# A forward transform folded at its thirds in an RWKV and Hyena kernel

## The chip, the cores and the metric

The kernel runs on one core of a Trainium2 chip. TensorE (PE) multiplies matrices into PSUM, VectorE (DVE), ScalarE (ACT) and GpSimd (POOL) do the elementwise work, and SyncE's queue (SP) issues the DMAs. The metric is the device time of one execution in microseconds (us); lower is better.

## The reference

Four sequences of 768 steps, 8 heads of 48 channels, so 384 channels in all. The first half is a linear recurrence with a decaying state per head:

```python
for t in range(S):
    cur = np.einsum('bhd,bhe->bhde', u[None] * kt, vt)
    y[:, :, t] = np.einsum('bhd,bhde->bhe', rt, state + cur)
    state = wt[:, :, :, None] * state + np.einsum('bhd,bhe->bhde', kt, vt)
```

Its output `x` (4 x 768 x 384) goes through a gated long convolution along the sequence, written with Fourier transforms:

```python
proj = x @ w_proj                      # three groups of 384 columns: x1, x2, x3
X2 = np.fft.rfft(x2, n=S, axis=1)
H = np.fft.rfft(filter_fft, n=S, axis=0)[None]
x2_conv = np.fft.irfft(X2 * H, n=S, axis=1)
return ((x1 * x2_conv * x3) @ w_out).astype(np.float32)
```

## The kernel before

**Recurrence.** Each sequence is cut into 6 chunks of 128 steps, 24 chunks in all. For a chunk, four loads bring `w`, `k`, `r`, `v` (192 KB each, rings of six buffers). ACT takes the logarithm (`lw`), PE sums it along the steps (`cs`, `ce`), ACT exponentiates (`en`, `enp`, `eq`, `eqp`). `q`/`qp` and `kh`/`khp` scale `r` and `k`; `tqk` transposes them on PE and `tT` copies them out; `sc` multiplies them, `mt` masks the result (or `ma` copies it and `mm` masks it on POOL). `kv` and `S` carry the state. The bonus term with `u` is `rk`, `rku`, a sum `cc` and a product `vc`. `y` collects the chunk's output in PSUM. It ends in one of two ways: `y` and then `xn`, in which DVE adds `vc`, or `yb`, in which a further matmul with the identity adds `vc` in PSUM, and then `xc`, a plain copy. `yt` transposes it and `xT` copies it to SBUF.

**Convolution.** The transform of 768 steps is split into halves first: `sa` and `sb` (lines 631 to 641) add and subtract chunk `ci` and chunk `ci` - 3, which gives a sum half and a difference half of 384 steps, kept with channels on the partitions in `sd_b`. `x2` (L679) projects each third (128 steps) of each half with `w_proj`; `ab` copies it to `ab_b`. `f` (L690) multiplies by the table `F` of sines and cosines, in six slots a sequence, three thirds a slot. Slots 0, 1, 4 and 5 are one group of 128 rows each and take one matmul of 384 columns per third; slots 2 and 3 hold two groups of 64 rows (`mid`) and take two half-wide matmuls per third. `da` and `db` (or a copy `X` and then `ua`, `ub`) multiply by the transformed filter, `pp` adds, `i1` and `i2` (L719) transform back, `ec`, `s`, `d` put the halves together (`d` writes its output backwards), `yy` multiplies by the gate. The gate is made from `p1`, `p3` (L648), `x1` and `g` or `gc` and `gm`. `po` (L761) multiplies by `w_out`, `o` copies, `st` stores.

**Set-up.** The filter is loaded once (`ldfilt`, 1152 KB), halved by `fs` and `fd` (L384 to L388) and transformed by `hf` with the helper `fwd` (L390), which `f` uses too; `rsc` (L339) scales a small table `rot`, on which the steps `ht` and `hr` wait. `z` and `zs` are matmuls on zeros whose result nobody reads.

**Order.** The whole program is one list, `ORDER` (L37). A word is an engine, an operation and its arguments, and for PE the PSUM bank: `P:f0.1@2` is `f` of sequence 0, slot 1, into bank 2, `A:ab0.1.2` a copy on ACT. Each engine runs its words in this order. A word can name DVE (`V`), ACT or POOL (`G`) for the same operation. A POOL word with "!" also waits for the latest DVE word whose operation is in the set `shut` (L803); this is called a turn below, and `rsc` is not in the set. Most operations run through helpers, so in the profile L231 is any copy on ACT and L232 any copy on another engine.

Of the kernel before, what the change touches and what calls it, by code (L numbers as in the profile page):

```python
# [37 lines left out]
S:ldw0 V:mem0 G:iorot! G:mke! G:iota! P:zs29@0 A:tLn S:ldw2 A:lw0 S:ldw1 S:ldr0 G:mki! S:ldk0 A:lw2  # L38
S:ldu V:mem2 V:mem4 V:mem3 V:ang1 V:mem1 V:ang2 V:ang0 A:lw1 V:angn P:cs0@0 P:ce0@1 P:z3@2 P:z7@3
A:enp0 P:ce1@2 S:ldfilt A:eq0 P:zs1@3 G:mkd! G:rk0! G:uc! S:ldk2 P:zs8@1 V:mem5 V:rku0 V:khp0 P:z2@3  # L40
P:cs1@1 A:sin P:cs2@4 P:z1@3 V:q0 S:ldk1 P:zs1@5 V:fs S:ldv0 A:enp2 A:ph1 A:enp1 P:zs2@3 P:zs2@5
P:tqk0@5 V:mem6 G:fd! P:hf0@3 V:rsc V:cc0 V:khp2 P:mtr0@0 P:hf1@4 A:tT0 A:ht0.0 P:ce2@5 P:sc0@8
# [6 lines left out]
V:mt2 A:lw5 A:ht2.1 A:xc1 V:cc3 P:ce5@2 V:S2 G:vc2! P:hf5@4 S:ldw6 S:ldv3 A:tT3 S:ldk5 S:ldr5
P:yb2@3 P:cs5@0 S:ldv4 G:q4! P:tqk4@5 V:hr2.0 V:hr2.1 P:sc3@8 V:xc2 A:v3 P:kv3@4 P:yt1@3 G:rk4!  # L50
G:vc3! G:rku4! A:eqp5 A:en5 S:ldw7 S:ldp1 A:tT4 A:lw6 A:xT1 A:v4 S:ldr6 G:kh5! P:zs2@0 A:xT0 G:rk5!
V:mt3 P:yb3@0 P:yt2@5 P:ce6@3 A:xc3 V:S3 P:sc4@8 A:eq6 A:lw7 V:cc4 G:vc4! V:qp5 P:tqk5@4 P:kv4@2
G:rku5! P:zs1@0 P:cs6@1 V:mt4 P:yt3@0 P:y4@3 A:tT5 V:S4 G:wc1! V:sa3 A:enp6 S:ldv5 A:xT3 A:xT2 V:xn4
P:sc5@8 S:ldk6 V:cc5 P:yt4@3 P:x20.0.0@4 G:q6! V:mt5 A:v5 V:sa4 P:ce7@5 A:ab0.0.0 V:khp6 G:vc5!
V:sb3 A:hb2 V:sb4 P:y5@2 G:rk6! S:ldw8 P:x20.0.1@4 S:ldr7 A:eq7 P:tqk6@1 A:lw8 P:x20.1.0@0 S:ldv6
V:xn5 P:cs7@5 P:yt5@2 A:ab0.0.1 P:x20.1.1@4 V:tT6 A:ab0.1.0 V:sa5 P:sc6@8 P:x20.0.2@0 A:xT4 P:cs8@3
V:sb5 A:v6 A:xT5 G:q7! G:rku6! A:ab0.0.2 P:ce8@1 S:ldk7 A:en7 A:en8 S:ldp0 A:ab0.1.1 P:f0.1@2
P:x20.1.2@0 G:rk7! V:mt6 S:ldk8 G:kh7! P:f0.0@5 A:ab0.1.2 V:cc6 V:db0.0 S:ldv7 A:eq8 V:rku7 P:kv6@4
P:f0.4@3 V:S6 P:f0.5@0 A:wc0 P:f0.2@1 G:vc6! G:kh8! V:da0.2 P:tqk7@4 V:db0.2 V:cc7 V:da0.0 G:v7!
S:ldr8 P:p10.1.0@3 G:rk8! P:p10.2.0@2 P:kv7@0 A:tT7 S:ldw10 A:x10.2.0 V:S7 P:sc7@8 P:p10.1.1@4  # L60
# [29 lines left out]
P:po0.4@1 A:eqp17 S:ldw23 S:st0.2 A:xT13 V:da1.2 A:o0.3 A:lw18 P:yt12@3 A:o0.4 A:xT12 P:sc16@8  # L90
V:qp17 P:f1.1@2 G:mm15! P:yt14@4 G:vc15! P:cs18@0 A:lw20 G:v16! G:kh17! V:S15 V:mt16 V:cc16 G:pp1.2!
S:ldr22 S:ldv20 P:yb15@5 G:rk17! S:ldr21 V:db1.0 S:st0.0 S:ldk22 P:tqk17@3 A:xT14 P:kv16@1 A:en18
A:xc15 P:p12.2.0@4 V:S16 A:tT17 P:p32.2.0@0 P:p12.0.0@2 P:ce18@1 P:sc17@8 P:yt15@3 A:x12.2.0
A:x12.0.0 A:eq18 P:ce20@4 V:pp1.0 V:pp1.1 V:rku17 V:sa15 A:v18 V:g2.2.0 G:kh18! G:vc16! A:xT15
A:eq20 P:p32.1.0@2 P:cs20@1 P:y16@5 P:i21.1@0 A:gc2.1.0 G:q18! P:p12.1.0@4 V:sb15 V:mt17 A:en20
A:v17 A:ec1.1 V:cc17 A:x12.1.0 V:gm1.1.1 V:q20 V:xn16 P:x22.1.0@2 P:i21.0@1 A:ec1.0 A:ab2.1.0
G:vc17! P:tqk18@0 P:i21.2@4 P:y17@1 V:tT18 V:xn17 G:kh20! P:kv18@5 V:S18 V:rk18 P:yt16@2 A:lw19
P:ce19@3 P:i11.0@0 A:ec1.2 P:yt17@1 A:xT16 A:eq19 P:cs19@4 V:sb16 A:en19 P:sc18@8 P:tqk20@3 V:d1.0
V:sa16 A:xT17 G:rku18! V:s1.0 A:v19 V:sb17 A:tT20 A:lw21 P:x22.1.1@4 P:i11.2@5 P:p32.1.1@2
G:gm1.2.1! V:sa17 A:gc2.1.1 V:d1.2 G:rk20! V:s1.2 P:p12.1.1@0 P:i11.1@3 V:mt18 A:ab2.1.1 G:q19!  # L100
P:x22.1.2@1 P:cs21@2 P:ce21@4 P:x22.0.0@5 G:kh19! A:x12.1.1 A:enp21 V:cc18 V:d1.1 A:eq21 A:ab2.0.0
A:lw22 A:ab2.1.2 P:x22.0.1@0 P:p32.0.0@4 V:s1.1 P:tqk19@5 P:p32.2.1@3 P:sc20@8 P:kv19@1 V:khp21
P:f2.5@2 V:g2.0.0 P:p12.0.1@4 A:ab2.0.1 G:vc18! G:rk19! P:x22.0.2@0 A:gc2.2.1 A:tT19 P:y18@5
A:x12.0.1 A:lw23 A:v20 S:ldr23 S:ldk23 P:f2.4@3 P:cs23@4 A:ab2.0.2 A:en23 V:yy1.0 V:yy1.2 V:yy1.1
V:S19 V:db2.2 V:mt20 P:ce22@1 P:po1.0@2 P:po1.4@0 A:eq22 P:sc19@8 G:rku19! P:cs22@1 G:q21! G:rku20!
S:ldv23 S:ldv21 A:o1.0 V:da2.2 V:cc19 P:tqk21@2 A:enp22 V:xn18 P:po1.2@3 G:rk21! P:po1.5@4 P:f2.1@5
V:khp22 S:ldv22 A:o1.4 P:yt18@1 P:po1.3@0 A:tT21 P:ce23@2 A:o1.2 P:kv20@3 G:q22! A:xT18 A:o1.5
# [25 lines left out]
def kernel(  # L133
# [506 lines left out]
    def op_sb(e, c):  # L640
        return two(e).tensor_sub(*sums(e, c, 1))  # L641
# [222 lines left out]
```

## Time and profile before

| | us |
|---|---|
| three runs | 160.06, 159.96, 159.25 |
| median | 159.96 |
| the profiled execution | 159.13 |
| its span, first to last instruction | 157.4 |

The profile is of one execution. Its page gives the busy time of each engine, the granted clock of PE in 40 slices of the span, the chain of work that ended last, and the costliest groups of instructions by line. A group's row reads: line, engine, operation, output and input with their shapes, count, busy us and mean ns of one, then idle time before them and what ended it. Rows of waits read: engine and line, what it waited for, us in total, how often, and the longest. Rows of the timeline and the chain begin with the start in us and the duration. PE's matmuls are pipelined, so the start of the next one tells more of their cost than the duration of one. In the first 30 us the 16 DMA engines were busy for 0.91 of the time.

### The profile page before, as it was taken

The numbers are of one execution on the slowest core, as the hardware profiler recorded it, in microseconds if no ns is written. First come the engines' busy times: TensorE is split into PE (matmuls) and PEld (weight loads), VectorE is DVE, ScalarE is ACT, GpSimd is POOL, SyncE is SP. The second block draws the span as 40 slices with busy tenths as digits, with TensorE's granted clock in tenths as the row PEclk, the third lists the DMA queues.
The fourth block names the chain that finished last, engine by engine and source line by source line (L and its number), as shares of the span: only waits on it lengthen the run. The fifth ranks groups of instructions, "written<-read, shape, count | busy, mean of one in ns | idle before, by whom it ended". The sixth has DMA issues, their size and how long they took to land.

```text
span 157.4 us, 4146 instructions
## 1 busy us (share of the span) xinstructions
PE 142.6 (91%) x1541; PEld 92.8 (59%) x1544; DVE 136.6 (87%) x264; ACT 126.0 (80%) x261; POOL 111.0 (71%) x134
## 2 busy tenths in 40 slices
...
PEclk9997559999999999999999999999999999999999
...
GB/s 102 203 277 184 215 170 201 209 251 191 236 210 145 265 160 213 186 203 218 179 252 189 158 205 196 187 226 216 218 138 200 0 4 2 0 0 4 329 240 233
...
## 3 DMA queue, kind: packets, MB, share of 16 engines
...
q8 instruction: 12, 0.20, 0.5%
q14 instruction: 8, 0.07, 0.1%
...
## 4 chain that ended last, share of the span: by engine, by line
PE 58%; ACT 10%; DVE 8%; DMA 8%; POOL 5%; issue 5%; SPq 3%; ACTq 0%; DVEq 0%; POOLq 0%
PE p L651 13%; PE x L682 6%; PE po L764 6%; DMA ldk<-in_k_dram 5%; PE f L402 5%; PE tqk L540 4%; PE i L722 4%; PE sc L553 3%; PE f L395 3%; SPq L450 2%; DMA ldw<-in_w_dram 2%; PE y L606 2%; PE ce L466 2%; DVE rot L340 2%; ACT xT L231 2%
## 5 line engine op out<-in xcount | busy, mean ns | idle before, releaser
L651 PE MATMUL p<-xT,wproj 128*128 128x384 bf16 x144 | 29.0, 326 | 0.0
L521 POOL TENSOR_TENSOR rk<-ldr,ldk 128x384 bf16<-128x384 f32 x23 | 23.0, 1002 | 7.4 <-DMA ldk<-in_k_dram 3.1
L560 DVE TENSOR_TENSOR mt<-sc,mask_excl 128x1024 bf16<-128x1024 f32 x22 | 26.7, 1216 | 0.5 <-PE sc L553 0.4
L231 ACT ACTIVATE qkT<-tqk 128x1024 bf16<-128x1024 bf16 x21 | 21.6, 1027 | 2.4 <-PE tqk L540 1.7
L534 POOL TENSOR_TENSOR vc<-v,cc 128x384 bf16<-128x384 bf16 x24 | 19.8, 831 | 3.8 <-ACT v L231 1.5
L518 POOL TENSOR_TENSOR qk<-ldr,eq 128x384 bf16<-128x384 f32 x17 | 17.0, 1001 | 3.0 <-ACT eq L485 3.0
L651 PEld LDWEIGHTS <-wproj 128*128 128x128 bf16 x144 | 12.8, 98 | 7.3 <-DVE sd L641 0.3
L540 PE MATMUL tqk<-ident,qk 128*128 128x128 bf16 x192 | 15.4, 223 | 1.1 <-DVE qk L502 1.1
L682 PE MATMUL x<-wproj,sd 128*128 128x384 bf16 x72 | 15.0, 326 | 1.0 <-ACT ab L231 0.6
L524 POOL TENSOR_TENSOR rku<-rk,u_bc 128x384 bf16<-128x384 bf16 x15 | 13.7, 915 | 2.7 <-DVE y L756 1.5
L722 PE MATMUL i<-m_b,P 128*128 128x384 bf16 x72 | 15.0, 326 | 0.0
L764 PE MATMUL po<-wout,y 128*128 128x384 bf16 x72 | 14.5, 326 | 0.5 <-DVE y L756 0.3
L540 PEld LDWEIGHTS <-qk 128*128 128x128 bf16 x192 | 12.1, 99 | 4.6 <-DVE qk L502 1.7
L456 ACT ACTIVATE lg<-ldw 128x384 bf16<-128x384 f32 x24 | 12.6, 524 | 2.5 <-DMA ldw<-in_w_dram 2.5
L514 POOL TENSOR_TENSOR qk<-ldk,en 128x384 bf16<-128x384 f32 x12 | 12.0, 1002 | 2.4 <-ACT x L231 2.0
L231 ACT ACTIVATE ab<-x 128x384 bf16<-128x384 f32 x24 | 11.4, 495 | 2.5 <-PE x L682 2.3
L527 DVE TENSOR_REDUCE cc<-rku 128x8 f32<-128x384 bf16 x24 | 12.9, 541 | 0.0
L231 ACT ACTIVATE x<-p 128x384 bf16<-128x384 f32 x24 | 11.6, 501 | 0.7 <-PE p L651 0.7
L231 ACT ACTIVATE xT<-yt 128x384 bf16<-128x384 bf16 x23 | 11.0, 494 | 1.0 <-DVE sd L638 0.8
L589 DVE TENSOR_TENSOR S<-kv,eq 128x384 bf16<-128x384 f32 x20 | 11.0, 550 | 0.8 <-PE kv L581 0.7
L710 DVE TENSOR_TENSOR UA<-f,T 128x768 bf16<-128x768 f32 x11 | 10.4, 949 | 0.3 <-PE f L395 0.3
L677 POOL TENSOR_TENSOR g<-g,x 128x384 bf16<-128x384 bf16 x8 | 7.2, 913 | 4.7 <-DVE g L677 2.6
...
## 6 DMA issues: line engine op xcount, KB each, us to landing
...
```

Source lines behind the costliest of these rows:

```text
L231: return nc.scalar.activation(out=o, in_=i, func=AF.Copy)
L518: return two(e).tensor_mul(qk_b[c % 3][:, 0, :, 0:D], ld["r"][c % LD], eq)
L521: return two(e).tensor_mul(rk_b[c % 2], ld["r"][c % LD], ld["k"][c % LD])
L524: return two(e).tensor_mul(rku_b[c % 2], rk_b[c % 2], u_bc)
L527: nc.vector.tensor_reduce(out=cc_b[c % 3], in_=rku_b[c % 2], axis=AX.X, op=ALU.add)
L534: return two(e).tensor_mul(vc_b[c % 3], v_b[c % 4], cc_b[c % 3].to_broadcast([L, H, D]))
L540: nc.tensor.transpose(p[:, x, j, :], qk_b[c % 3][:, x, 2 * j:2 * j + 2, :], ident)
L560: nc.vector.tensor_mul(mt_b[c % 3], bank_of[f"sc{c}"].rearrange("p q j t -> p (q j) t"), dataclasses.replace(m[:, :], ap=[m[:, :].ap[0], [ ...
L651: nc.tensor.matmul(p, wproj[:, n, cb, fb * L:(fb + 1) * L], xT_b[b % 2][:, cb, sl], start=(cb == 0), stop=(cb == CB - 1),)
L682: nc.tensor.matmul(p, sd_b[q][:, cb, ti * L:(ti + 1) * L], wproj[:, 1, cb, :], start=(cb == 0), stop=(cb == CB - 1),)
L722: nc.tensor.matmul(p, P_b[b % 2][:, s // 2, s % 2, cb * L:(cb + 1) * L], m_b[:, s].rearrange("p a t -> p (a t)"), start=(i == 0), stop=(i ...
L764: nc.tensor.matmul(p, y_b[0][:, cb, ti * L:(ti + 1) * L], wout[:, cb, :], start=(cb == FIRST[0]), stop=(cb == FIRST[-1]),)
```

## The change

The sines and cosines of a half sequence are symmetric or antisymmetric about its middle. So the first third and the mirrored last third are added (`fp`) or subtracted (`fm`) before the projection; slots 0, 2 and 5 need the sum, slots 1, 3 and 4 the difference, and all need the middle third as it is. `x2` still makes three products a half: sum, middle, difference. `f` then takes two of them a slot instead of three. `sa` and `sb` of a sequence's last chunk write their 128 steps backwards, so that `fp` and `fm` read plain slices.

```diff
+    fo_b = ring("fo", 2, [L, 2, CB, L], BF16)
...
+    EVEN = (0, 2, 5)
...
-        return sd_b[q][:, :, (ci - NT) * L:(ci - NT + 1) * L], lo, hi
+        o = sd_b[q][:, :, (ci - NT) * L:(ci - NT + 1) * L]
+        if ci == NCH - 1:
+            o = dataclasses.replace(
+                o, offset=o.offset + (L - 1) * o.ap[-1][0],
+                ap=list(o.ap[:-1]) + [[-o.ap[-1][0], L]],
+            )
+        return o, lo, hi
...
+    def op_fp(e, b, q):
+        return two(e).tensor_add(
+            fo_b[q][:, 0], sd_b[q][:, :, 0:L], sd_b[q][:, :, 2 * L:3 * L],
+        )
+
+    def op_fm(e, b, q):
+        return two(e).tensor_sub(
+            fo_b[q][:, 1], sd_b[q][:, :, 0:L], sd_b[q][:, :, 2 * L:3 * L],
+        )
...
             nc.tensor.matmul(
-                p, sd_b[q][:, cb, ti * L:(ti + 1) * L], wproj[:, 1, cb, :],
+                p, sd_b[q][:, cb, L:2 * L] if ti == 1 else fo_b[q][:, ti // 2, cb, :],
+                wproj[:, 1, cb, :],
                 start=(cb == 0), stop=(cb == CB - 1),
             )
...
     def op_f(e, b, s, bank):
-        fwd(f"f.{b}.{s}", bank, s, ab_b[0][:, 0], ab_b[0][:, 1])
+        p = ps(f"f.{b}.{s}", bank)
+        side = 0 if s in EVEN else 2
+        for ti, j in ((1, 1), (0, side)):
+            if s in (2, 3):
+                for q in (0, 1):
+                    nc.tensor.matmul(
+                        p[DP * q:DP * q + DP, :], mid(ti, s, q), ab_b[0][:, q, j, :],
+                        start=(ti == 1), stop=(ti == 0),
+                    )
+            else:
+                nc.tensor.matmul(
+                    p, slot_cols(ti, s), ab_b[0][:, s // 4, j, :],
+                    start=(ti == 1), stop=(ti == 0),
+                )
...
     shut = {"kh", "q", "rk", "rku", "vc", "v", "ua", "ub", "pp", "yy", "gm", "wc",
-            "fs", "fd", "hb", "ang", "angn", "he", "uc"}
+            "fs", "fd", "hb", "ang", "angn", "he", "uc", "rsc", "fp", "fm"}
```

The whole of `ORDER` is written anew, 1088 words before and 1094 after: another order on every engine, other banks, and other engines for some operations. The words whose number on an engine differs, without those where two engines only differ by one:

| operation | before | after |
|---|---|---|
| `fp`, `fm` | none | 11 DVE, 5 POOL |
| `yb` with `xc`; `y` with `xn` | 9; 15 | 16; 8 |
| `xc` | 8 ACT, 1 DVE | 16 ACT |
| `rku` | 9 DVE, 15 POOL | 16 DVE, 8 POOL |
| `rk` | 1 DVE, 23 POOL | 3 DVE, 21 POOL |
| `q`, `qp` | 2 and 5 DVE, 17 POOL | 3 and 1 DVE, 20 POOL |
| `eq`, `eqp` (both ACT) | 19, 5 | 23, 1 |
| `xT` | 1 DVE, 23 ACT | 4 DVE, 20 ACT |
| `g`; `gc` with `gm` | 12 DVE; 12 ACT, 4 DVE and 8 POOL | 14 DVE; 10 ACT, 5 DVE and 5 POOL |
| `o` | 2 DVE, 22 ACT | 24 ACT |
| `mc` | 3 DVE | 1 DVE, 2 ACT |
| `fd` | POOL | DVE |
| `z`, `zs` matmuls | 21, 46 | 7, 33 |

The loads begin in another order: before `ldw0 ldw2 ldw1 ldr0 ldk0 ldu ldfilt ldk2 ldk1 ldv0`, after `ldw1 ldw2 ldw0 ldu ldfilt ldk1 ldr1 ldk0 ldv0 ldr0`. On DVE, `rsc` and `fd` follow `fs` directly, and `rk1`, `q1` and `rku1` stand among the set-up that comes next.

More of the change, by code (lines that the diff above doesn't have):

```diff
@@ L37 @@
 ORDER = """
[L38 to L42, printed above, removed]
@@ L49 @@
[L49 to L54, printed above, removed]
@@ L55 @@
[L55 to L60, printed above, removed]
@@ L90 @@
[L90 to L95, printed above, removed]
@@ L96 @@
[L96 to L107, printed above, removed]
@@ L126 @@
-V:d3.1 P:poa3.5@2 P:poa3.2@4 A:o2.3 P:poa3.1@5 S:st2.5 V:yy3.1 P:pob3.5 P:pob3.0 P:pob3.2 P:poa3.4@1
-S:st2.0 P:poa3.3@3 A:o3.5 P:pob3.3 P:pob3.4 S:st2.1 S:st2.4 S:st2.3 A:o3.0 S:st3.5 V:o3.2 S:st3.0
-S:st3.2 P:pob3.1 A:o3.1 A:o3.4 A:o3.3 S:st3.1 S:st3.4 S:st3.3
+S:ldw1 S:ldw2 G:iota! G:mki! G:iorot! S:ldw0 A:tLn A:lw2 V:mem3 V:mem1 G:mke! A:lw1 V:ang1 S:ldu
+V:ang2 V:ang0 V:mem0 V:angn V:mem4 P:cs2@0 V:mem6 P:ce2@1 S:ldfilt A:en2 P:zs29@2 A:lw0 P:ce1@2
+G:uc! G:mkd! V:mem5 V:fs S:ldk1 A:sin S:ldr1 S:ldk0 S:ldv0 S:ldr0 P:z7@0 P:zs2@0 P:ce0@3 P:hf0@0
@@ new lines @@
+P:cs1@4 V:rsc P:zs2@5 P:cs0@5 A:eq1 A:en1 A:eq0 A:ht0.1 A:v0 P:hf1@2 V:fd S:ldr3 P:hf2@4 P:hf3@3
+A:enp0 A:ht0.0 V:rk1 V:q1 V:mem2 V:hr0.1 A:ht1.1 G:kh1! V:khp0 V:hr0.0 P:kv0@5 S:ldk3 V:hr1.1 G:q0!
+A:eqp2 P:tqk0@0 V:S0 P:hf4@5 A:ht1.0 G:rk0! S:ldw3 V:rku1 P:tqk1@4 S:ldk2 S:ldr2 A:he P:hf5@2 G:rk3!
+A:lw3 A:ph2 V:tT0 P:ce3@0 V:cc1 S:ldv1 V:rku0 A:ht2.1 S:ldw4 A:tT1 V:hr1.0 V:cc0 P:cs3@3 P:sc0@8
+G:kh2! V:hr2.1 G:vc0! P:mtr1@4 V:qp2 P:tqk2@1 G:rk2! A:enp3 A:ht2.0 A:ms1 V:mt0 A:v1 S:ldw5 S:ldv2
+P:kv1@5 A:tT2 V:rku3 V:rku2 V:hr2.0 P:sc1@8 P:mtr0@1 P:yb0@2 S:ldr4 S:ldk4 A:lw4 A:eq3 G:hb2! V:khp3
@@ new lines @@
+P:yb4@2 P:yt3@5 P:yt2@4 G:rk6! A:lw8 A:xc4 P:ce7@1 V:S4 A:xT2 V:mt5 A:eq7 V:sa3 V:sb3 A:xT3 G:vc5!
+P:y5@0 V:xn5 P:ce8@2 P:yt4@4 A:wc1 P:yt5@0 G:kh6! V:sb4 V:sa4 A:eq8 G:rku6! P:tqk6@5 V:sb5 V:sa5
+A:xT5 A:en7 P:x20.1.1@1 S:ldv6 P:x20.0.1@2 G:v6! A:hb1 S:ldk7 V:fp0.1 P:x20.1.0@0 V:fm0.0 V:fp0.0
+S:ldr7 A:ab0.0.1 A:ab0.1.1 A:ab0.1.0 V:fm0.1 S:ldp0 P:x20.0.2@3 P:x20.0.0@2 V:tT6 A:ab0.0.2 V:cc6
+G:rk7! A:ab0.0.0 P:sc6@8 P:kv6@0 P:f0.5@1 P:cs8@3 P:x20.1.2@2 V:q7 V:rku7 A:xT4 V:db0.2 G:kh7! A:wc0
+P:f0.0@4 P:f0.2@5 S:ldk8 A:en8 G:vc6! P:tqk7@1 S:ldr8 G:q8! G:rk8! A:ab0.1.2 A:tT7 P:p10.2.1@3
@@ new lines @@
+P:po0.2@2 A:o0.5 V:da1.2 G:rk17! P:f1.3@4 P:f1.2@5 A:tT16 P:sc15@8 G:q17! S:ldk22 P:yb14@3 S:ldv21
+S:ldk21 P:kv16@0 A:lw18 A:o0.4 G:rku17! G:vc16! S:ldv19 S:ldv20 P:ce18@1 A:ma15 P:sc16@8 V:da1.1
+V:db1.1 A:lw19 P:po0.3@5 G:mm15! A:xc14 P:yt14@3 P:ce19@4 V:mt16 V:xT14 A:eq18 A:o0.2 P:po0.0@1
+A:o0.3 V:S16 G:vc15! G:v17! P:f1.1@2 P:tqk17@5 P:p12.0.0@3 A:lw20 V:db1.0 P:yb15@0 A:o0.0
+P:p12.2.0@1 G:q18! S:ldr22 V:gm1.1.1 S:ldv23 S:st0.4 A:eq19 P:cs18@2 P:cs20@4 V:rk18 A:tT17
+A:x12.0.0 P:sc17@8 V:pp1.1 P:yb16@3 A:enp18 V:pp1.0 S:st0.1 V:pp1.2 V:rku18 A:xc15 A:en20 V:khp18
```

123 lines of the change are left out of this document (70 added, 53 removed).

## The prediction

> **What bounds the kernel now.** I read the page first, then the busy time in three stretches, then each engine's waits inside the middle one, then the start.
>
> ```profile
> span 157.4 us, 4146 instructions
> PE 142.6 (91%) x1541; PEld 92.8 (59%) x1544; DVE 136.6 (87%) x264; ACT 126.0 (80%) x261; POOL 111.0 (71%) x134
> PEclk9997559999999999999999999999999999999999
> PE 58%; ACT 10%; DVE 8%; DMA 8%; POOL 5%; issue 5%; SPq 3%; ACTq 0%; DVEq 0%; POOLq 0%
> ...
> 0.00:30.00 30.00, 21.94 (x199) 14.18 (x202) 19.73 (x53) 19.97 (x36) 14.47 (x30) 0.83 0.91 195
> 30.00:140.00 110.00, 108.39 (x1272) 72.06 (x1274) 106.37 (x193) 98.85 (x210) 93.17 (x103) 1.00 0.79 169
> 140.00:157.40 17.40, 12.30 (x75) 6.59 (x71) 10.46 (x20) 7.19 (x16) 3.32 (x3) 0.99 0.50 182
> ```
>
> The columns of the last three rows are stretch, length, busy time of PE, PEld, DVE, ACT and POOL, then granted clock, DMA share and GB/s. The chain of work that ended last is 58% PE, so at first sight a matmul saved is time saved. The middle stretch says otherwise: of 110 us DVE is busy 106.37, ACT 98.85 and POOL 93.17. PE's 108.39 is modelled and hides small gaps. DVE has 110 - 106.37 = 3.6 us to give; no saving on PE can bring more in this stretch unless DVE's own work falls.
>
> POOL looks free with 17 us idle. Its waits and DVE's rows in the same stretch show that it is not:
>
> ```profile
> POOL rk L521 <- DVE y L756: 2.7, 1, 2.7
> POOL g L677 <- DVE rku L524: 2.1, 1, 2.1
> POOL qk L514 <- ACT x L231: 2.0, 1, 2.0
> ...
> L756 DVE TENSOR_TENSOR y<-SD,g 128x768 bf16<-128x768 bf16 x8 | 4.2, 558 | 0.0
> L716 DVE TENSOR_TENSOR P<-UA,UB 128x768 bf16<-128x768 bf16 x6 | 3.1, 552 | 0.0
> L524 DVE TENSOR_TENSOR rku<-rk,u_bc 128x384 bf16<-128x384 bf16 x5 | 1.8, 353 | 0.0
> L677 DVE TENSOR_TENSOR g<-g,x 128x384 bf16<-128x384 bf16 x3 | 1.0, 349 | 0.0
> ```
>
> The first two waits are for DVE instructions whose result POOL does not use: the program makes each POOL word marked "!" wait for the latest DVE instruction of the set `shut` (a turn). The four DVE groups, in the same window, take 4.2 + 3.1 + 1.8 + 1.0 = 10.1 us, so POOL and turns hold 93.17 + 10.1 = 103.3 of 110 us. PE, DVE and POOL-with-turns are all at 94% or more.
>
> The start is different: there single waits are long.
>
> ```profile
> 15.31 2.61 POOL L388 TENSOR_TENSOR UA<-filt 128x1152 bf16<-128x1152 f32 x1 [4.51 <-DVE UA L385]
> 15.38 2.56 DVE L340 TENSOR_TENSOR rot<-rot,rsc 128x12 f32<-128x12 f32 x1
> ...
> DVE UA L385 <- DMA filt<-in_moe_filter_fft_dram: 1.7, 1, 1.7
> ACT E L420 <- DVE rot L340: 4.2, 1, 4.2
> L323 DVE TENSOR_SCALAR o<-tcol 128x3 int32<-128x3 f32 x1 | 0.2, 169 | 0.0
> ```
>
> Twelve elements took 2.56 us, while a POOL instruction of 2.61 us had begun 0.07 us earlier. The nearest small DVE row, 169 ns, says what `rot` costs alone.
>
> **The change part by part.** Durations, from the groups by line and the chain in order of time:
>
> ```profile
> 137.19 0.49 PE f L402 x3
> 138.65 0.61 PE f L395 x6
> ...
> L395 PE MATMUL f<-ab,F 128*64 128x384 bf16 x48 | 5.4, 334 | 0.0
> L598 PE MATMUL y<-vc,ident 128*128 128x384 bf16 x9 | 3.0, 328 | 0.3 <-POOL vc L534 0.3
> L638 DVE TENSOR_TENSOR sd<-xT,yt 128x384 bf16<-128x384 bf16 x12 | 4.1, 350 | 0.4 <-ACT eq L485 0.2
> L618 DVE TENSOR_TENSOR xn<-y,vc 128x384 bf16<-128x384 f32 x15 | 8.2, 550 | 0.8 <-PE y L606 0.7
> L385 DVE TENSOR_TENSOR UA<-filt 128x1152 bf16<-128x1152 f32 x1 | 1.4, 1359 | 1.7 <-DMA filt<-in_moe_filter_fft_dram 1.7
> L231 ACT ACTIVATE xn<-y 128x384 bf16<-128x384 f32 x8 | 4.0, 495 | 0.2 <-PE y L606 0.2
> L231 ACT ACTIVATE xT<-yt 128x384 bf16<-128x384 bf16 x23 | 11.0, 494 | 1.0 <-DVE sd L638 0.8
> L524 POOL TENSOR_TENSOR rku<-rk,u_bc 128x384 bf16<-128x384 bf16 x15 | 13.7, 915 | 2.7 <-DVE y L756 1.5 <-DVE rk L521 0.6 <-DVE g L677 0.5
> L641 POOL TENSOR_TENSOR sd<-xT 128x384 bf16<-128x384 bf16 x1 | 0.9, 910 | 0.1
> L753 DVE TENSOR_TENSOR SD<-i,E 128x384 bf16<-128x384 f32 x12 | 6.6, 552 | 0.3 <-issue 0.3
> L744 DVE TENSOR_TENSOR SD<-i,E 128x384 bf16<-128x384 f32 x12 | 6.6, 550 | 0.0
> L508 DVE TENSOR_TENSOR qk<-ce,ldr 128x384 bf16<-128x384 f32 x5 | 2.7, 548 | 0.0
> L518 POOL TENSOR_TENSOR qk<-ldr,eq 128x384 bf16<-128x384 f32 x17 | 17.0, 1001 | 3.0 <-ACT eq L485 3.0
> ...
> 133.51 0.87 ACT L231 ACTIVATE xT<-yt 128x384 bf16<-128x384 bf16 x2
> ```
>
> *PE.* Three full `f` matmuls take 0.49, so one is 0.163; sixteen go (four slots of four sequences, one each): 2.6 us. Six half-wide ones take 0.61, so a pair is 0.20; eight pairs go: 1.6 us. The new order also makes `yb` of seven more `y`: seven bonus matmuls at 0.163, +1.1. Net -3.1 us of PE time, spread evenly.
>
> *DVE.* Counted from the two orders. In: eleven folds (`fp`, `fm`) at 0.35, as `sd`, 3.9; seven `rku` from POOL, 2.5; `fd` 1.36; `rk`, `q`, `xT`, `g`, `gm`, `ub` about 4.7. Out: seven `xn` at 0.55, 3.9; four `qp` 2.2; one `mt` 1.2; `da`, `o`, `xc`, `ec`, `sa`, `mc`, `ms`, `hb` about 4.8. Net +0.3 us: nothing. `rot` loses its 2.4 us beyond, in the start.
>
> *ACT.* Eight more `xc` 4.0, three fewer `xT` -1.5, and single moves of `mc`, `ms`, `wc`, `ma`, `o`, `ec`, `X`, `v` against two `gc`: +7.6 us of isolated durations; about +6 where they run back to back (two `xT` take 0.87, not 0.99). 98.85 + 6 of 110 still fits.
>
> *POOL.* Seven `rku` (-6.4), `fd` (-2.6), `gm`, `rk`, `wc` out; five folds at 0.91 (+4.6), `q`, `sa`, `mm` in: about -4.9. Against it stand new turns: eleven folds, seven `rku` and three `rk`/`q` on DVE, 3.9 + 2.5 + 1.65 = 8.0 us. POOL with turns: about +3.
>
> *The reversed sums.* `sa`/`sb` of the last chunk, eight instructions, write backwards. Before has a reversed write in `d` and a forward one in `s`, each 0.55, but with a float32 input. Bounds: 0 and 8 x (0.55 - 0.35) = 1.6 us; I take 0, since the `d` row is the nearest. [...]
>
> *Start.* `fd` goes to DVE, behind `rsc`: `rot` is no longer beside a POOL instruction, -2.4 us on DVE. `filt` is issued behind `u` and three `ldw`; `ldr0` and `ldk0` (0.39 MB; at the stretch's 195 GB/s, 2.0 us) come after it, so the transform of the filter starts earlier by up to 1.7 us, its DMA wait. The price: chunk 0's `k` and `r` come later, behind 1.2 MB, and POOL, DVE and PE stand without inputs until then; the chain's DMA piece at the start can grow by as much:
>
> ```profile
> 5.85 8.59 DMA ldk<-in_k_dram
> ```
>
> Fourteen of 21 `z` matmuls go; the clock was already at 0.5 in the two slices where the filter transform ran (PEclk), so they did not hold it up: 0, at worst +3 us if half clock lasts until 30. Ends of the start: -4.1 and +3; I take -1.5, the `rot` row less what late inputs give back.
>
> *Middle.* PE -2.1 (three of four sequences, less most bonus matmuls), DVE 0, ACT +5, POOL with turns +3. Ends: -3.1 and +3; I take -0.5, near to DVE, which changes least and idles least.
>
> *Tail.* The last sequence's `f` is 4 x 0.163 + 2 x 0.20 = 1.05 us shorter on the chain; between `sb` and `x2` a fold is new, 0.35 on DVE or 0.91 on POOL, which has three of the four there. `x2` of the middle third needs no fold and goes first, which hides part. Ends -1.05 and +0.9; I take 0.
>
> Sum: -1.5 - 0.5 + 0 = -2.0. The profiled execution took 159.13 us (157.4 span, 1.7 around it): 157.1. It lies 0.6 under the mean of the three runs (159.76; their median is 159.96), so **157.7**.
>
> **The rivals.** *More is kept (155.2).* The start gives 3, and DVE uses most of its 3.6 us of idle middle because PE is never late: -4.5. For it: DVE's waits in the middle are mostly for PE, the longest sum being that of `S`:
>
> ```profile
> DVE S L589 <- PE kv L581: 0.7, 3, 0.3
> ```
>
> Against: DVE's work is unchanged.
>
> *No change (159.7).* Late inputs eat the start's gain, and PE's saved time becomes waits for DVE. For it: DMA share 0.91 in the first 30 us. Against: ACT alone waited 4.2 us for `rot`, and that wait goes.
>
> *Slower (161.7).* The added two-input DVE instructions meet running POOL instructions as `rot` did. Place: folds and `rku` in the middle. Price: an unlucky one waits about half a POOL instruction of 1 us (`q`, L518), 0.5 us on DVE; eight of the 21 make 4 us; less the 2 us gain above, +2. It decides from four collisions on (2 us). For it: the row of `rot`. Against: before's `rku`, `y`, `P` show almost none (353, 558, 552 ns), so turns work as ordered. [...]
>
> *The fold isn't done* (counts unchanged): under 1%, the loop is written for two thirds.
>
> **How the numbers follow.** Forecast 0.42 (156.3 to 159.1), more 0.20, no change 0.20, slower 0.18. A measurement can tell about 0.5% (0.8 us) from no change, so faster means under 159.16: 0.40 + 0.20 = 0.60; same 0.21; slower 0.19. The range takes in the first three and the lower half of the slower one: 155.0 to 161.2.
>
> **What would show it.** [...]
>
> [...]
>
> I am wrong if the start is not shorter, if POOL's turns grow past 5 us, or if ACT passes DVE.

## The result, and the profile after

| | before | after |
|---|---|---|
| median of 20 runs each, us | 159.66 | 159.32 |
| lowest to highest, us | 158.37 to 160.37 | 156.95 to 160.97 |
| profiled execution, us | 159.13 | 159.96 |
| its span, us | 157.4 | 158.3 |

The ratio of after to before is 0.9929, with a 95% interval of 0.9900 to 0.9957: by it the change saves 0.7%, about 1.1 us, where the sum of the prediction was 2.0. The ratio counts only executions within 1.5% of their kernel's fastest, which are all of before's but nine of after's 20, the profiled one not among them; the medians of all 20 lie only 0.3 us apart. So the saving is 0.3 to 1.1 us, by how it is counted.

The head of the page of after, in the order used for before:

```profile
span 158.3 us, 4054 instructions
PE 136.4 (86%) x1492; PEld 89.0 (56%) x1492; DVE 134.1 (85%) x271; ACT 131.2 (83%) x274; POOL 107.5 (68%) x130
PEclk9999999999789999999999999999999999999998
PE 40%; ACT 14%; DMA 13%; DVE 13%; SPq 9%; issue 4%; POOL 4%; ACTq 0%; POOLq 0%; DVEq 0%
```

PE is busy for 6.2 us less, and its share of the chain that ended last falls from 58% to 40%. DMA and SP's queue together now hold 22% of it, ACT 14%. This share is a loose figure: the three kernels below that differ from after in their loads alone show 41% to 54% for PE. The first two of the three stretches, with the same columns:

```profile
0.00:30.00 30.00, 19.48 (x217) 13.29 (x217) 20.82 (x57) 23.67 (x44) 15.54 (x32) 1.00 0.92 194
30.00:140.00 110.00, 103.56 (x1198) 68.55 (x1196) 101.96 (x196) 97.95 (x208) 86.06 (x94) 0.98 0.79 169
```

In the middle every engine has more idle time than before: DVE 8.0 us in place of 3.6, POOL 23.9 in place of 16.8. No engine is at its limit over the whole stretch (DVE, the busiest but PE, is at 93%). The instructions that the prediction priced, from the groups by line and by form:

```profile
L720 PE MATMUL f<-ab,F 128*128 128x384 bf16 x32 | 7.7, 326 | 0.0
L715 PE MATMUL f<-ab,F 128*64 128x384 bf16 x32 | 3.6, 334 | 0.0
L342 DVE TENSOR_TENSOR rot<-rot,rsc 128x12 f32<-128x12 f32 x1 | 0.2, 164 | 0.0
L646 DVE TENSOR_TENSOR sd<-xT,yt 128x384 bf16<-128x384 bf16 x11 | 3.7, 344 | 0.0
L649 DVE TENSOR_TENSOR sd<-xT,yt 128x384 bf16<-128x384 bf16 x11 | 3.7, 348 | 1.9 <-ACT xT L233 1.9
L652 DVE TENSOR_TENSOR fo<-sd 128x384 bf16<-128x384 bf16 x5 | 1.8, 361 | 0.0
L657 DVE TENSOR_TENSOR fo<-sd 128x384 bf16<-128x384 bf16 x6 | 2.4, 399 | 0.0
```

The parts behaved as priced: `f` went from 48 to 32 matmuls of each kind, `rot` from 2.56 to 0.16 us, the folds (`fo`) take 361 and 399 ns.

To see where the time went I cut every execution at two marks, the `sc` of chunk 6 (where the first convolution begins) and that of chunk 23 (the last chunk). From the timelines of before and then of after:

```profile
43.98 0.40 PE L553 MATMUL sc<-qkT 48*128 48x128 bf16 x8
128.97 0.40 PE L553 MATMUL sc<-qkT 48*128 48x128 bf16 x8
```

```profile
45.73 0.40 PE L555 MATMUL sc<-qkT 48*128 48x128 bf16 x8
129.45 0.40 PE L555 MATMUL sc<-qkT 48*128 48x128 bf16 x8
```

So the start grew by 1.7 us (44.0 to 45.7), the stretch between the marks shrank by 1.3 (85.0 to 83.7), and the tail grew by 0.4 (28.4 to 28.85). Across the two orders the marks do not fall at the same work (ahead of the first one before has four `x2` products and after five; behind the second one before has three `p1` and after six), so this split is exact only between kernels of one order. What holds the start stands in the chain of after, in order of time (start, duration):

```profile
34.63 5.85 DMA o<-in_moe_w_proj_dram
40.50 1.17 ACT wproj L233
41.72 4.08 PE x L700 x15
45.80 0.33 PE sc L555 x8
```

After reached the `sc` of chunk 5 at 36.1 us, 3.0 ahead of before (39.1). Before needs 4.9 us from there to the `sc` of chunk 6, after 9.6. Of these 4.7 us more, 1.2 are PE's wait at the first `x2`, which needs the `x2` third of `w_proj`. That load left SP at 34.63 where before issued it at 30.29, since the new order puts 31 loads ahead of it and the old one 27. Another 1.5 us come with the clock: in this execution it was granted at 0.50 from 42 to 44 us and at 0.81 from 44 to 46, and the fifteen `x2` matmuls took 0.27 us each in place of 0.163. The rest, about 2 us, is other work that the new order has in this place (a fifth `x2` product, a `yb`, two `yt`) and short waits.

### The profile page after: what moved, and what is told of

It is laid out like the page before. It is cut to its first block, busy times and chain, and to the rows that moved or that the text cites. A ratio compares the mean times of both kernels' runs of the same rounds, so it can differ in the third digit from the quotient of the medians.

```text
span 158.3 us, 4054 instructions
## 1 busy us (share of the span) xinstructions
PE 136.4 (86%) x1492; PEld 89.0 (56%) x1492; DVE 134.1 (85%) x271; ACT 131.2 (83%) x274; POOL 107.5 (68%) x130
## 4 chain that ended last, share of the span: by engine, by line
PE 40%; ACT 14%; DMA 13%; DVE 13%; SPq 9%; issue 4%; POOL 4%; ACTq 0%; POOLq 0%; DVEq 0%
SPq L452 9%; PE p L669 8%; PE x L700 7%; PE po L796 5%; DMA o<-in_moe_w_proj_dram 4%; DMA ldw<-in_w_dram 4%; DMA ldr<-in_r_dram 3%; ACT qkT L233 3%; PE f L720 3%; PE tqk L542 3%; DMA ldv<-in_v_dram 2%; PE sc L555 2%; PE i L754 2%; PE f L715 2%; DVE UA L742 2%
## 5 line engine op out<-in xcount | busy, mean ns | idle before, releaser
L669 PE MATMUL p<-xT,wproj 128*128 128x384 bf16 x144 | 29.6, 326 | 0.9 <-ACT qkT L233 0.9
L523 POOL TENSOR_TENSOR rk<-ldr,ldk 128x384 bf16<-128x384 f32 x21 | 21.3, 1018 | 6.2 <-DMA ldr<-in_r_dram 2.0
L562 DVE TENSOR_TENSOR mt<-sc,mask_excl 128x1024 bf16<-128x1024 f32 x21 | 25.5, 1213 | 0.0
L520 POOL TENSOR_TENSOR qk<-ldr,eq 128x384 bf16<-128x384 f32 x20 | 20.1, 1004 | 2.9 <-ACT eq L487 1.1
L754 PE MATMUL i<-m_b,P 128*128 128x384 bf16 x72 | 14.0, 325 | 0.0
L233 ACT ACTIVATE xT<-yt 128x384 bf16<-128x384 bf16 x20 | 10.1, 513 | 2.7 <-DVE sd L646 2.3
L462 PE MATMUL cs<-lg,mask_incl 128*128 128x384 bf16 x24 | 7.6, 331 | 5.5 <-ACT lg L458 5.1
L745 DVE TENSOR_TENSOR UB<-f,T 128x768 bf16<-128x768 f32 x11 | 10.3, 949 | 2.0 <-PE f L720 2.0
L487 ACT ACTIVATE eq<-ce 128x392 f32<-128x392 f32 (+1 forms) x23 | 11.6, 507 | 0.2
L233 ACT ACTIVATE v<-ldv 128x384 bf16<-128x384 f32 x19 | 10.4, 545 | 1.2 <-DMA ldv<-in_v_dram 1.2
```

Source lines behind the costliest of these rows:

```text
L233: return nc.scalar.activation(out=o, in_=i, func=AF.Copy)
L520: return two(e).tensor_mul(qk_b[c % 3][:, 0, :, 0:D], ld["r"][c % LD], eq)
L523: return two(e).tensor_mul(rk_b[c % 2], ld["r"][c % LD], ld["k"][c % LD])
L562: nc.vector.tensor_mul(mt_b[c % 3], bank_of[f"sc{c}"].rearrange("p q j t -> p (q j) t"), dataclasses.replace(m[:, :], ap=[m[:, :].ap[0], [ ...
L669: nc.tensor.matmul(p, wproj[:, n, cb, fb * L:(fb + 1) * L], xT_b[b % 2][:, cb, sl], start=(cb == 0), stop=(cb == CB - 1),)
L754: nc.tensor.matmul(p, P_b[b % 2][:, s // 2, s % 2, cb * L:(cb + 1) * L], m_b[:, s].rearrange("p a t -> p (a t)"), start=(i == 0), stop=(i ...
```

## The experiments

Each ratio is against runs of before on the same chip and is counted as the one above; beside it stand the medians of all executions of the kernel and of before. The last four columns are of the profiled execution: up to the `sc` of chunk 6, from there to that of chunk 23, from there to the end, and the span.

| kernel | ratio | 95% interval | medians, us | start | middle | tail | span |
|---|---|---|---|---|---|---|---|
| before | 1 | | | 44.0 | 85.0 | 28.4 | 157.4 |
| after | 0.9929 | 0.9900 to 0.9957 | 159.32 / 159.66 | 45.7 | 83.7 | 28.8 | 158.3 |
| new order, w_proj earlier | 1.0009 | 0.9977 to 1.0041 | 160.01 / 159.46 | 46.4 | 82.9 | 28.8 | 158.1 |
| new order, PE kept busy | 0.9969 | 0.9936 to 1.0002 | 159.62 / 159.46 | 43.8 | 83.9 | 28.9 | 156.6 |
| new order, `fd` on POOL | 0.9952 | 0.9919 to 0.9985 | 158.70 / 159.46 | 45.3 | 83.7 | 28.8 | 157.8 |
| new order, no fold | 1.0362 | 1.0311 to 1.0414 | 164.59 / 159.46 | 45.3 | 86.3 | 30.3 | 161.9 |
| old order, two thirds | 0.9826 | 0.9794 to 0.9858 | 156.70 / 159.29 | 44.4 | 82.9 | 27.9 | 155.2 |
| old order, fold put in | 1.0736 | 1.0685 to 1.0788 | 171.14 / 159.29 | 48.2 | 91.5 | 30.7 | 170.4 |
| new order, one matmul a slot | 0.9969 | 0.9942 to 0.9997 | 159.10 / 159.29 | 46.4 | 83.6 | 28.6 | 158.6 |
| new order, lighter loads | 0.9907 | 0.9867 to 0.9947 | 158.08 / 159.29 | 44.8 | 82.5 | 29.2 | 156.5 |
| old order, `rot` early | 1.0002 | 0.9971 to 1.0034 | 159.08 / 159.11 | 42.4 | 85.8 | 28.4 | 156.6 |
| new order, early `v` left out | 0.9846 | 0.9816 to 0.9876 | 156.60 / 159.11 | 42.5 | 83.9 | 29.1 | 155.5 |
| new order, tiny folds | 1.0092 | 1.0058 to 1.0126 | 160.48 / 159.11 | 45.6 | 84.4 | 29.2 | 159.2 |
| new order, tiny `xc` | 0.9952 | 0.9917 to 0.9987 | 158.71 / 159.11 | 44.0 | 84.1 | 28.8 | 156.9 |

The stretches are of one execution each. The four kernels of the new order whose middle has the same work as in after (w_proj earlier, PE kept busy, `fd` on POOL, early `v` left out) show 82.9 to 83.9 there, so a difference of half a microsecond in a stretch means little.

### The start: `rot` alone, in the old order

```diff
- ... V:fs S:ldv0 A:enp2 ... G:fd! P:hf0@3 V:rsc V:cc0 ...
+ ... V:rsc V:fs S:ldv0 A:enp2 ... G:fd! P:hf0@3 V:cc0 ...
```

> The kernel of before with one word moved: rsc, which scales the twelve elements of rot, stands ahead of fs instead of behind the start of fd on POOL, so that it takes about 0.16 us in place of 2.56. Nothing else differs. By the prediction's start step the 2.4 us on DVE come through less what late inputs give back: 1.5 us under before, 157.9 where before takes 159.4. Rival (the start is paid back at the next wait, since each later stage waits for loads and not for rot): 159.0 to 159.5.

Measured: 159.08 us beside 159.11, ratio 1.0002. The step did what it should and yet brought nothing. From the timeline, then from the chain of the same kernel, then from POOL's timeline, where the brackets hold the wait ahead of the instruction:

```profile
11.46 0.17 DVE L340 TENSOR_TENSOR rot<-rot,rsc 128x12 f32<-128x12 f32 x1
```

```profile
33.23 6.61 DMA ldk<-in_k_dram
```

```profile
39.90 1.00 POOL L521 TENSOR_TENSOR rk<-ldr,ldk 128x384 bf16<-128x384 f32 x1 [0.33 <-DMA ldk<-in_k_dram]
41.34 1.00 POOL L518 TENSOR_TENSOR qk<-ldr,eq 128x384 bf16<-128x384 f32 x1 [0.44 <-DMA ldr<-in_r_dram]
...
55.83 1.00 POOL L518 TENSOR_TENSOR qk<-ldr,eq 128x384 bf16<-128x384 f32 x1 [0.67 <-DMA ldr<-in_r_dram]
```

The `sc` of chunk 5 came at 36.0 us, 3.1 us ahead of before. Then a load of `k` that landed at 39.84 was late, and at chunk 6 the lead was 1.6 us. Between 39.9 and 55.8 us POOL waited five times for loads of `k` and `r`, 2.0 us together, where before had no such wait; by the `sc` of chunk 9 (62.0) the lead was 0.9. Of it 0.8 us was left at the end of the profiled execution, nothing that the runs could tell. The rival's account holds: up to 56 us, most of what was computed sooner was then waited for at loads.

### The start: does the wait for w_proj hold it?

Moving that load forward alone, from behind `ldw8` to behind `ldv4`:

```diff
- ... S:ldv4 S:ldr6 ... S:ldw8 S:ldp1 ...
+ ... S:ldv4 S:ldp1 S:ldr6 ... S:ldw8 ...
```

> The new kernel with one load moved: the part of w_proj that the first projection x2 needs is issued four loads (768 KB, at 200 GB/s 3.9 us) earlier, about where the old order had it; the loads it overtakes come 576 KB later. If the late weight is what ate the earlier start, PE begins the first x2 near 39 to 40 us instead of 41.7 and the whole is 1 to 2 us faster than the new kernel, ratio to before about 0.983 to 0.987. If the load stream as a whole is the limit (every load moved ahead only pushes others back), the loads overtaken are waited for instead and the ratio stays at 0.990 to 0.996.

Measured: 160.01 us, ratio 1.0009, if anything slower than after. The load was issued at 31.15, 3.5 us sooner, and `x2` began at 43.35, 1.6 us later. From ACT's timeline:

```profile
40.20 0.52 ACT L458 ACTIVATE lg<-ldw 128x384 bf16<-128x384 f32 x1 [3.19 <-DMA ldw<-in_w_dram]
...
42.12 1.18 ACT L233 ACTIVATE wproj<-o 128x1152 bf16<-128x1152 f32 x1
```

The load of `w` that had been pushed back now held ACT for 3.19 us, and the cast of `w_proj` stood behind it in ACT's order. Here the load that went ahead pushed another one back. So the next kernel made the stream of loads shorter instead:

```diff
- ... S:ldv3 ... S:ldv5 ... S:ldv4 ...
-        return copy(e, v_b[c % 4], ld["v"][c % LD])
+        return copy(e, v_b[c % 4], ld["v"][c % 3 if c < LD else c % LD])
```

> The new order without the loads of v of chunks 3 to 5 (these multiply by v of chunks 0 to 2, so that part is not computed): 0.59 MB, about 2.9 us at 200 GB/s, go from the load stream ahead of w_proj, whose last third landed at 40.5 us in after and held the first x2. Theory L (the start's gain is lost waiting for w_proj): x2 begins 2 to 3 us earlier and it comes through to the end, 155.5 to 157 where before takes 159.4 and after about 158.3. Theory X (no single wait; the next late thing takes its place): 157.8 to 158.8.

Measured: 156.6 us, ratio 0.9846, whose interval lies wholly under that of after. The chain of this kernel:

```profile
38.78 1.16 ACT wproj L233
39.98 2.60 PE x L700 x15
42.58 0.33 PE sc L555 x8
```

`x2` began 1.7 us sooner than in after and took 2.60 us instead of 4.08; the middle and the tail stayed as they were. The lead of 3.2 us at chunk 6 (of which 1.5 us goes with the clock, granted at 1.00 from 40 to 50 us here and at 0.83 in after) ended as 2.8 us in the span, 1.3 us between the ratios (0.9929 - 0.9846 = 0.0083 of 159) and 2.2 between the medians, each taken as a ratio to before's. Theory L held in its time, though it had `x2` begin 2 to 3 us sooner. It cannot be said how much of it came through `w_proj` and how much through the other loads behind it.

### The start: the filter's difference half on POOL, and the clock

```diff
- ... V:fs S:ldk1 ... V:rsc ... V:fd S:ldr3 ...
+ ... V:fs G:fd! S:ldk1 ... V:rsc ... S:ldr3 ...
-            ... "hb", "ang", "angn", "he", "uc", "rsc", "fp", "fm"}
+            ... "hb", "ang", "angn", "he", "uc", "fp", "fm"}
```

> The new kernel with the start's gain undone: fd is on POOL again, beside rsc on DVE. rot should take about 2.5 us again. If the start carries through to the end, as the prediction had it, the time rises by 1.5 to 2.5 us and the ratio to before is 1.002 to 1.009. If what comes after waits for loads in any case, the time changes by less than 0.5 us and the ratio stays at 0.990 to 0.996.

Measured: 158.7 us, ratio 0.9952, no different from after. `rot` ran before `fd` began and took 0.16 us, but another DVE instruction now ran beside `fd`. From DVE's timeline and then POOL's:

```profile
13.96 2.98 DVE L520 TENSOR_TENSOR qk<-ldr,eq 128x384 bf16<-128x384 f32 x1
```

```profile
13.58 2.94 POOL L390 TENSOR_TENSOR UA<-filt 128x1152 bf16<-128x1152 f32 x1 [4.30 <-DVE rot L342]
```

The same `qk` took 0.55 us in after. Those 2.4 us put the first `sc` back by 1.2 us (22.37 beside 21.14), and by chunk 5 the two stood at 36.34 and 36.12: here a loss of the start was swallowed, as the gain of `rot` alone had been.

Seven matmuls on zeros (three and four) in the gap ahead of `x2`, to see what half clock costs:

```diff
- ... P:yt4@4 A:wc1 ... P:tqk6@5 V:sb5 ...
+ ... P:yt4@4 P:z3@1 A:wc1 ... P:tqk6@5 P:z4@1 V:sb5 ...
```

> The new kernel with seven matmuls on zeros put back (128x512, 0.21 us each, 1.5 us of PE) just before the first x2, where the profile shows PE poorly filled and then 15 x2 matmuls of 0.27 us in place of 0.163. If the missing warm-up matmuls cost the clock there, the granted clock of 40 to 50 us rises from 0.83 to 1.00, x2 is 1.5 us shorter, the spread of the runs shrinks and the ratio to before is 0.983 to 0.988. If x2 is bound by its inputs anyway, or the clock falls for other reasons, the ratio stays at 0.990 to 0.998.

From the timeline of this kernel, and of after for comparison:

```profile
41.28 1.14 PE L700 MATMUL x<-wproj,sd 128*128 128x384 bf16 x6
```

```profile
41.72 2.08 PE L700 MATMUL x<-wproj,sd 128*128 128x384 bf16 x6 [1.16 <-ACT wproj L233]
```

The granted clock was 1.00 from 30 to 48 us and chunk 6 came at 43.8 instead of 45.7, with the middle and tail of after: that execution is 158.54 us. Yet the ratio, 0.9969 (0.9936 to 1.0002), is not under that of after. In the execution of after with the lower clock the first fifteen `x2` matmuls took 4.0 us up to the `sc` of chunk 6, here 2.5, but these rows don't show that the median suffers from it. Nor do they show that the zeros kept the clock up. With `fd` on POOL the kernel has no such matmuls, PE waited even longer at `x2` (1.53 us), and the granted clock stayed at 1.00:

```profile
40.00:42.00 2.00, 1.03 (x13) 0.68 (x12) 2.00 (x8) 0.90 (x3) 1.43 (x2) 1.00 0.91 192
42.00:44.00 2.00, 1.23 (x8) 0.78 (x8) 1.51 (x4) 2.00 (x5) 0.62 (x1) 1.00 0.66 113
```

### The middle: the fold taken out of the new order

The code of before for `sums`, `x2` and `f`, with the order of after; `fp` and `fm` are dropped, and three pairs of `x2` and `ab` words (a slot needs all three thirds again) move ahead of the first `f` that reads them.

```diff
- ... V:fp0.1 P:x20.1.0@0 V:fm0.0 V:fp0.0 ... P:f0.5@1 ... P:x20.1.2@2 ... A:ab0.1.2 ...
+ ... P:x20.1.0@0 ... P:x20.1.2@2 A:ab0.1.2 P:f0.5@1 ...
-        p = ps(f"f.{b}.{s}", bank)
-        ...
+        fwd(f"f.{b}.{s}", bank, s, ab_b[0][:, 0], ab_b[0][:, 1])
```

> The new order without the fold: no fp and fm, sums written forwards, three matmuls a slot; three copies ab and two projections x2 move a few places so that each f has its inputs. PE has 4.2 us more work, DVE 3.9 us and POOL 4.6 us less. If PE bounds the middle, this is 2.5 to 4 us slower than the new kernel, ratio to before 1.008 to 1.018. If DVE and POOL bound it, as the prediction had it, it is equal or up to 2 us faster, ratio 0.98 to 0.994.

Measured: 164.59 us, ratio 1.0362. Beside after, the middle is 2.6 us longer and the tail 1.5: within this order the fold is worth 4.1 us in these two stretches and, by the ratios, 0.0433 of 159 or 6.9 us (5.4 by the medians), although without it DVE and POOL have sixteen instructions less. Beside before, the same kernel is 5.8 us slower by its ratio. So the fold pays for all of PE's 4.2 us, and what surrounds it in the new order costs most of that. The order was not written for this kernel, so the second number is no price of the order by itself.

### The middle: PE's time alone

```diff
-        fwd(f"f.{b}.{s}", bank, s, ab_b[0][:, 0], ab_b[0][:, 1])
+        for ti in (0, 1):
+            ...
+                    p, slot_cols(ti, s), ab_b[0][:, s // 4, ti, :],
+                    start=(ti == 0), stop=(ti == 1),
```

> The order of before, with f summing the first two thirds only; the last third is left out of the transform and nothing is folded, so DVE, ACT, POOL and the queues have exactly the work of before and PE has 4.2 us less. Theory V (the prediction's: DVE and POOL with its turns bound the middle): 0.5 us in the middle and 1 us in the tail, 158.0 to 159.0 beside a before of 159.5. Theory P (PE bounds nearly everywhere): all 4.2 us, 155.3. Theory D (the loads set the pace until the last one lands near 113 us): only what f of the last two sequences saves, 2.1 us, 157.4.

Measured: 156.7 us beside 159.29, ratio 0.9826: 2.8 us of the 4.2 come through, 2.1 in the middle and 0.5 in the tail of the profiled execution. Theory V is ruled out in its size (0.5 to 1.5) and theory P in its own (4.2). Theory D's figure, 157.4, is nearest, though the saving was not in the tail, where D had half of it. Theory V's reason is not ruled out. Between the marks, in before and then in this kernel:

```profile
43.98:128.97 84.99, 84.35 (x989) 56.37 (x988) 82.15 (x147) 78.36 (x165) 71.90 (x80) 1.00 0.85 181
44.35:127.27 82.92, 81.99 (x965) 54.51 (x964) 81.85 (x147) 78.12 (x165) 71.45 (x80) 1.00 0.90 188
```

DVE's work stayed the same, and its idle time fell from 2.8 to 1.1 us. The saving of 2.1 fits under the prediction's cap, by which PE can bring no more than DVE has idle. That DVE is what stopped it is not shown, since no kernel here takes work from DVE in the middle of the old order.

The same in the new order, one third fewer again:

```diff
-        for ti, j in ((1, 1), (0, side)):
+        for ti, j in ((0, side),):
```

> The new order with f taking one matmul a slot; the middle third is left out of the transform. PE has another 4.2 us less, every other engine has the work of after. Theory V: at most 1.5 us under after (158.3 where before takes 159.5 and after 158.4 to 159.3): 157.5. Theory P: 4.2 us under after, 154.5 to 155. Theory D: about 2.1 us under after, 157.

Measured: 159.1 us, ratio 0.9969 (0.9942 to 0.9997), not under after, and the middle is 83.6 against 83.7. Here 4.2 us of PE bring nothing: once the fold has taken its share, what is late next is not PE.

### The middle: DVE and POOL, ACT, and the loads

```diff
-            fo_b[q][:, 0], sd_b[q][:, :, 0:L], sd_b[q][:, :, 2 * L:3 * L],
+            fo_b[q][:, 0, 0, 0:2], sd_b[q][:, 0, 0:2], sd_b[q][:, 0, 2 * L:2 * L + 2],
```

> The new order, with fp and fm adding and subtracting two elements a partition instead of 384, so the fold's sums are left out while its instructions, turns and waits stay: about 3.4 us less on DVE and 4.3 less on POOL. Theory V (DVE and POOL with its turns bound the middle): 2 to 3 us under after, 155.5 to 156.5 where before takes 159.4. Theory X (a chain over all engines, none of them bound): 0.3 us a sequence where x2 waits for a fold, 157.3 to 158.3.

```profile
L654 DVE TENSOR_TENSOR fo<-sd 128x2 bf16<-128x2 bf16 x5 | 1.0, 196 | 0.0
L659 DVE TENSOR_TENSOR fo<-sd 128x2 bf16<-128x2 bf16 x6 | 0.9, 150 | 0.0
L289 DVE MEMSET fo<- 128x384 uint32 x2 | 0.8, 378 | 0.1
```

Measured: 160.48 us, ratio 1.0092, slower than after. The two memsets that fill `fo` put the filter transform back by 0.8 us (`fs` at 12.85 instead of 12.06); the rest of the 2.6 us between the ratios (1.7 between the medians) I cannot place. From chunk 6 on the kernel has 2.3 us less of folds on DVE and 3.5 less on POOL, and its middle is 84.4, not shorter than 83.7. The expectation of 3.4 us on DVE was too high, as a fold of two elements still took 150 to 196 ns here. The folds' work on DVE and POOL does not bound the middle of the new order.

```diff
-        copy(e, xn_b[c % 3], bank_of[f"y{c}"].rearrange("p h d -> p (h d)"))
+        copy(e, xn_b[c % 3][:, 0:2], bank_of[f"y{c}"].rearrange("p h d -> p (h d)")[:, 0:2])
```

> The new order, with xc copying two elements a partition instead of 384, so that the output of sixteen chunks is left out of the convolution: about 0.3 us less for each, 4.7 us less on ACT, which is what the new order had put on it. Theory A (ACT binds the new order, so PE's saved time went there): 2 us or more under after, 156.3 or less where before takes 159.4. Theory X: ACT is late in a few places only, 157.3 to 158.3.

```profile
L233 ACT ACTIVATE xn<-y 128x2 bf16<-128x2 f32 x16 | 2.9, 179 | 0.1
```

Measured: 158.71 us, ratio 0.9952, no different from after, with a middle of 84.1. ACT lost 5.1 us (8.0 to 2.9 for its sixteen `xc`; three memsets of 0.2 us are new on DVE) for nothing, so theory A falls.

```diff
- ... S:ldv6 ... S:ldv7 ... S:ldv23 ...
```

> The new order without the 18 loads of v from chunk 6 on (each such chunk multiplies by an earlier chunk's v, so the computation is left out in part): 3.5 MB less, about 17.7 us of the load stream at 200 GB/s, with no engine's work changed. Theory D: the stalls of 30 to 50, 70 to 80 and 100 to 110 us (6.3 us of PE idle) shrink, 153 to 156 beside a before of 159.5. Theories P and V: the loads are not what is waited for, 158 to 159.5.

```profile
90.00:100.00 10.00, 10.00 (x138) 6.83 (x135) 10.00 (x19) 9.65 (x23) 7.51 (x10) 1.00 1.03 255
100.00:110.00 10.00, 8.31 (x91) 5.22 (x90) 7.77 (x19) 7.70 (x15) 7.04 (x8) 1.00 0.01 4
```

Measured: 158.08 us, ratio 0.9907, no different from after by the intervals. The loads now end near 100 us instead of after 110, and the middle is 1.2 us shorter (82.5), though kernels with an unchanged middle went down to 82.9. Of these cuts it is the only one that shortens it. The thin spot from 100 to 110 us, in which PE is busy for 8.3 of 10, stands there without any load. In after its chain runs over ACT and DVE:

```profile
103.25 0.92 ACT qkT L233
104.17 0.39 ACT xT L233
...
104.86 0.55 DVE cc L529
105.40 0.47 DVE SD L785
...
108.51 0.91 ACT qkT L233
```

From 100.02 to 112.05 us it holds sixteen pieces of ACT and eight of DVE, nearly back to back, and none of PE: the transposed `q` and `k` of a chunk wait their turn on ACT behind `ec`, `xT` and `x1` copies. No engine's work, cut by 2 to 5 us, and no lighter load stream shortened the new order's middle by more than 1.2.

### The fold put into the old order

Before's order, with `fp` and `fm` set behind the last sums of each half, `x2` of the middle third first, and words moved back only where a product would have been read too soon.

```diff
- ... V:sb3 A:hb2 V:sb4 ... P:x20.0.1@4 ... P:x20.1.0@0 ... V:sa5 ... V:sb5 ...
+ ... V:sb3 A:hb2 V:sb4 ... V:sa5 V:fp0.0 V:fm0.0 ... V:sb5 V:fp0.1 V:fm0.1 ...
```

> The order of before with the whole fold put into it by hand: the reversed sums, sixteen fp and fm on the engines on which the new order has them, x2 of the middle third moved ahead, f with two matmuls a slot; nothing else is moved. Theory V: DVE has 3.9 us more where it had 3.6 us to give, so no gain or a loss, 159 to 162 beside 159.5. Theory P: the 4.2 us of PE less what the folds hold x2 up (about 0.35 us a half sequence), 155.5 to 157. Theory D: 157.5 to 159.

Measured: 171.14 us, ratio 1.0736, 12 us slower than before, far outside every theory. All three stretches grew, the middle by 6.5 us. A piece of its chain in the third sequence, without its rows of `issue` of under 0.1 us:

```profile
111.04 0.66 PE x L701 x3
111.72 0.49 ACT ab L234
112.21 0.39 ACT xT L234
112.62 0.37 DVE sd L650
113.06 1.09 POOL fo L653
114.20 0.86 PE x L701 x3
```

Nothing is at its limit here; the chain hops from PE to ACT, DVE, POOL and back, and PE's queue stands meanwhile. Without the fold, two of a sequence's six `x2` products (the first third of each half) can run once chunk 3 is summed, and two more after chunk 4. With it four of the six need a fold, and so the sums of chunk 5. That is a price of the fold that the prediction did not name: not its instructions but when their results exist. How much of the 12 us it is, no run here shows, for two other things came with it. From 44 to 48 us the granted clock was 0.50, and six `x2` matmuls took 2.04 us from 46.15 to the next `sc`, 0.34 each in place of 0.163. And four groups of DVE adds and products took 3.5 us more than in before (`y`, `P`, `g` and `rku`, 15.4 to 18.9 us together), `y` above all, in before and then here:

```profile
L756 DVE TENSOR_TENSOR y<-SD,g 128x768 bf16<-128x768 bf16 x11 | 5.8, 557 | 0.1
L789 DVE TENSOR_TENSOR y<-SD,g 128x768 bf16<-128x768 bf16 x11 | 7.6, 719 | 0.1
```

The prediction's slower rival had named such longer DVE instructions, beside running POOL ones; what these ran beside is not shown by the means. Of the kernels here that compute everything, none is faster than after beyond the intervals.

## Why the prediction came out as it did

The range (155.0 to 161.2) held, but it also took in no change and half of the slower rival, so that says little. The direction held by the ratio; by the medians the 0.3 us lie under the 0.8 that the prediction itself calls no change. The sum, -2.0, was made of terms that missed in both directions, so that it came within 1 or 2 us is partly luck. In the stretches of after with a full clock (the kernel with PE kept busy) the start is -0.2, the middle -1.1, the tail +0.4, together -0.8; the ratio gives -1.1.

- **Start, -1.5: this step failed.** Its parts came true: `rot` lost 2.4 us, `filt` was used 1.8 us sooner (12.06 instead of 13.87), and the `sc` of chunk 2 came at 27.94 in place of 28.71, 0.8 us ahead, that of chunk 5 3.0 ahead. But "the `rot` row less what late inputs give back" gave back all of it: with `rot` alone the gain is 0, give or take half a microsecond. The price of the late inputs was weighed for chunk 0's `k` and `r`; it was paid later, at `w_proj` in after and at the loads of `k` and `r` from 40 to 56 us with `rot` alone. The rival "no change" had this half right.
- **Middle, -0.5, near to DVE: too small, and the reason fails in the new order.** In the old order PE's saving brought 2.1 between the marks, within DVE's idle time there (2.8), so half a microsecond was too little, but the cap held. In the new order DVE in the middle stood at 93%, where it was at 97% in before, and making the folds tiny brought nothing. By the kernel without the fold, the fold brought 2.6 in the middle and the surrounding order took 1.3 back.
- **Tail, 0.** Measured +0.4. The fold brings 1.5 there (30.3 to 28.8), more than the 1.05 priced; the order takes 1.9.
- **ACT +6, POOL -4.9, DVE nothing.** Busy times changed by +5.2, -3.4 and -2.4 (`rot` among the last). ACT did not pass DVE, and making it lighter changed nothing: hidden, as taken. In the middle POOL's waits for DVE grew by about 2 us (from 9.3 to 11.7, the sum of its rows of waits), with 7 us less of work: under the 5 that would have made me wrong.
- **z warm-ups, 0.** The first 30 us had a mean granted clock of 0.83 before and now have 1.00. A dip came later, to 0.50 at the first `x2`, and went with 1.5 us more in the execution that shows it; in the medians it isn't seen.
- **Reversed sums, 0: right.** 344 and 348 ns in groups that hold reversed and forward ones, and no single row on DVE is above 0.36 us.
- **Collisions, the slower rival: it did not come in the new order.** `fm` averages 399 ns because one of six took 0.65; all eleven folds together lost 0.4 us. Where a collision was provoked (`qk`, 2.98 us beside POOL's `fd`), it cost what `rot` had cost (2.4 us each), and the end did not move. In the old order with the fold put in, `y` grew from 557 to 719 ns on average; whether by collisions was not shown.

What stays open: which of the new order's choices takes back the 3 us beside the fold, whether an order for three thirds could be as good as that, and why the executions of after spread over 4.0 us where those of before spread over 2.0.
